# Softplus of the first two hidden tiles moved into the attention's list, splits and evictions reordered at a group change, and the last outputs written in another row order

## Chip, cores, metric

One core of a Trainium2 chip. The time is that of the device, in microseconds, from the start of the program to its end; a time below is the median of three runs. The engines named are PE (TensorE matmul) with its weight loads (PEld), DVE (VectorE), ACT (ScalarE), POOL (GpSimd) and SP (SyncE, which here issues nearly all the transfers).

## What is computed

```python
# q, k, v: 4 batches x 8 heads x 576 x 64, s: 4 x 8 x 576
scores = (q @ k.T) / 8 + min(-(cum[i] - cum[j]), 0)   # cum: running sum of max(s, 0)
x = softmax(causal(scores)) @ v                       # -> 2304 tokens x 512
h = x @ w_in;  x = softplus(h) @ w_out                # 512 -> 2048 -> 512
x = x / sqrt(mean(x * x) + 1e-6) * rms_g
g = x @ w_gate;  val = x @ w_val                      # 512 -> 1536
out = (g * sigmoid(g) * val) @ w_out2                 # 1536 -> 512, 2304 x 512 fp32
```

The products are kept near fp32 accuracy: an operand is split into a part `hi` rounded to fp32r and a rest `lo`, and a product is three matmuls (hi·hi, hi·lo, lo·hi). So every operand of TensorE costs one ACT copy (hi) and one subtraction on DVE or POOL (lo).

## The kernel before

**Three stages.** Attention runs over 16 pairs of heads. The first MLP runs over six tiles of 384 tokens and 16 slices of 128 hidden columns, 96 steps in all (`STEPS`, line 171). The second MLP runs over three groups of 768 tokens (two tiles of 384) and 12 slices of hidden columns, 36 steps in all; step n has group g = n // 12 and slice f = n % 12.

**Order of work.** Each engine takes its instructions strictly in the order in which they are written. For the attention that order comes from a planner: `attention_ops` (line 617) lists operations with engine, estimated duration and dependences, and `attention_order` (line 716) takes again and again the one that can start earliest, ties going to the lower rank (pair times a period plus an offset from the table `OFF`). The list ends with `H0` and `H1`, the first matmuls of the first MLP (`m1_h(0)`, `m1_h(1)`, lines 792 to 794), which write two PSUM banks of the attention's pool. From there on the order is a list of (time, function) pairs sorted by time. In it step i of the first MLP has `m1_h` (matmuls), `m1_sp` (two softplus activations of the same bank, `l` in fp32, line 813, and `gh` rounded, line 814), `m1_gl` (`gl` = `l` - `gh` on DVE, line 818) and `m1_y` (matmuls into four banks, line 830). The PSUM pool of the attention is closed and another opened in its place, so the banks of `y` lie over banks that the attention used.

**A step of the second MLP** is `m2_g(n)` (line 992). Gate and value of two token tiles are a 2 by 2 block product, made with seven products instead of eight (`prod`, six matmuls each, lines 979 to 981) in two PSUM banks D and A, in the order A12·B21 (D), A11·B11 (A), S2·T2 (A), S1·T1 (D), S3·T3 (A), S4·B22 (D), A22·T4 (A). The banks are read in between (`c1`, `u2`, `m5` on ACT; `gA`, `vB`, `gB` and the product with `s0` on DVE, line 1052), and the first product into a bank of the next step has to wait for the last read of it. The gated result is split by `m2_hi` (ACT, line 985) and `m2_lo` (DVE, line 990). `m2_out(n - 1, 0)` and `m2_out(n - 1, 1)` (line 1071, nine matmuls each) add the step before to six output banks: rows m = 0 to 2 of 128 tokens, then m = 3 to 5. `u_split` (lines 924, 925) splits the weights of the next step, one ACT copy and one POOL subtraction for each of four pieces. `u_load(n + 2)` (line 913) issues four loads on SP for the step after it; a load waits until POOL has done with the tile that it overwrites.

**At a group change** two things come on top. The seven token-side operands of the new group (B21, B11, T2, T1, T3, B22, T4, each in two halves j) are split by `n_split` (line 961): an ACT copy (line 968) and a subtraction (line 970), which is on POOL for an odd index and on DVE for an even one, so that of T1 the half j = 0 is POOL's and j = 1 DVE's. "ahead" is the last step of a group (n = 11, 23), "fresh" the first of the next (n = 12, 24). And the six output banks of the old group are copied out and stored by `m2_evac` (two copies of 256 columns and two stores on SP for each m). Its tiles in the first two groups are `yt`, of which there are seven that go round in order, `y_tile` at line 833. Before, the copies of m = 1, 3, 5 are ACT's (line 1082) and those of m = 0, 2, 4 DVE's (line 1084); rows 0 to 2 are copied in the fresh step, rows 3 to 5 in the one after it.

**At the end** `m2_end` (line 1087) adds the last two steps to the outputs and stores them, rows 0 to 2 first. There the even m use tiles `gl`, of which there are three.

Of the kernel before, what the change touches and what calls it, by code (L numbers as in the profile page):

```python
# [8 lines left out]
F32 = mybir.dt.float32  # L9
F32R = mybir.dt.float32r  # L10
# [5 lines left out]
ALU = mybir.AluOpType  # L16
# [96 lines left out]
    "X1": -56.86,  # L113
    "X2": 52.29,
    "X3": -59.99,
    "H0": -23.02,
    "H1": -64.43,
}
CONV0 = 7.439
CONVR = 1.0130  # L120
# [25 lines left out]
def attention_moe_kernel(ctx, tc, q, k, v, s, w_in, w_out, w_gate, w_val, w_out2, rms_g, out):  # L146
    nc = tc.nc
    B, H, S, D = q.shape
# [3 lines left out]
    P = 128  # L152
    NP = B * H // 2
    NH = B * H
    HP = H // 2
    KD = DM // P
    T = 384
# [8 lines left out]
    NA = 2 * FA  # L166
    CONV = [(1, c) for c in range(NA)]
    NG = NT // (2 * T)
    NS2 = NG * F2
    N5 = 3  # L170
    STEPS = [(t, t, f) for t in range(NTILE) for f in range(FA)]
# [8 lines left out]
    pools = {}  # L180
# [4 lines left out]
    def ps_p(name):  # L185
        return pools["ps"].tile([P, 512], F32, tag="p", name=name, bufs=2)
# [7 lines left out]
    def f32(ap):  # L194
        return ap.bitcast(F32)
# [96 lines left out]
    st = {}  # L292
# [324 lines left out]
    def attention_ops():  # L617
        ops, names = [], {}

        def op(name, eng, dur, fn, deps, base, lat=None, alloc=(), mode=""):  # L620
            if lat is None:
                lat = 0.3 if eng == "PE" else 0.15
            names[name] = len(ops)
            ops.append(dict(name=name, eng=eng, dur=dur, fn=fn, deps=deps, base=base, lat=lat, alloc=alloc, mode=mode))
# [82 lines left out]
            op((f"X{a}", 0), "DVE", 0.8, lambda a=a: x_split(0, a, nc.vector), [("XL", 0), ("QT1", NP - 1)] + [(f"X{a - 1}", 0)] * (a > 0), NP)  # L707
        for i in range(2):
            op((f"H{i}", 0), "PE", 2.1, lambda i=i: m1_h(i),
               [(f"X{a}", 0) for a in range(KD)] + [("MT", NP - 1), ("CL", NA - 1), ("CP", len(CONV) - 1)] + [("R" + x, p) for x in "abcd" for p in (NP - 2, NP - 1)], NP, mode="f")  # L710
        for o in ops:
            o["deps"] = [names[d] for d in o["deps"]]
            o["alloc"] = [(t, [names[r] for r in rd]) for t, rd in o["alloc"]]
# [92 lines left out]
    def m1_tile(tag, bufs, dt=F32):  # L806
        return pools["m1"].tile([P, T], dt, tag=tag, name=tag, bufs=bufs)

    def m1_sp(i):
        h = st.pop(("h", i))  # L810
        l = st["l", i] = m1_tile("l", 2)
        gh = st["gh", i] = m1_tile("gh", 3, F32R)
        nc.scalar.activation(out=l, in_=h, func=AF.Softplus)
        nc.scalar.activation(out=gh, in_=h, func=AF.Softplus)  # L814

    def m1_gl(i):
        gl = st["gl", i] = m1_tile("gl", 3, F32R)
        nc.vector.tensor_tensor(out=gl, in0=st.pop(("l", i)), in1=f32(st["gh", i]), op=ALU.subtract)  # L818

    def m1_y(i):  # L820
# [152 lines left out]
    def prod(o, n, wn, xn, start, stop):  # L973
        wh, wl = st["W", n, wn]
        for j in range(2):
            xh, xl = st["X", xn, j]
            c = slice(j * P, (j + 1) * P)
            first, last = start and j == 0, stop and j == 1
            nc.tensor.matmul(o, wh[:, c], xh, start=first, stop=False, skip_group_check=True)  # L979
            nc.tensor.matmul(o, wh[:, c], xl, start=False, stop=False, skip_group_check=True)  # L980
            nc.tensor.matmul(o, wl[:, c], xh, start=False, stop=last, skip_group_check=True)  # L981

    def m2_hi(n, h):
        gh, l = st["g", n][0], st["lt", n, h]
        nc.scalar.activation(out=gh[:, h * T:(h + 1) * T], in_=l, func=AF.Copy)

    def m2_lo(n, h):
        (gh, gl), l = st["g", n], st.pop(("lt", n, h))
        c = slice(h * T, (h + 1) * T)
        nc.vector.tensor_tensor(out=gl[:, c], in0=l, in1=f32(gh[:, c]), op=ALU.subtract)  # L990

    def m2_g(n, fill=None):
        g, f = divmod(n, F2)
        D, A = ps_p("D")[:, 0:T], ps_p("A")[:, 0:T]
        c1, u2, m5 = [m1_tile("gh", 3) for _ in range(3)]
        gA, s0, gB = [m1_tile("gl", 3) for _ in range(3)]
        s1, vB = m1_tile("u", 1), m1_tile("l", 2)
        st["g", n] = [pools["m1"].tile([P, 2 * T], F32R, tag="xb", name="gg", bufs=4) for _ in range(2)]
        tt, act = nc.vector.tensor_tensor, nc.scalar.activation
        ahead = f == F2 - 1 and g < NG - 1  # L1000
        fresh = f == 0 and g > 0

        def renew(go, *names):
            if go:
                for nm in names:
                    for j in range(2):
                        n_split(g + ahead, j, nm)

        prod(D, n, "A12", "B21", True, True)
        prod(A, n, "A11", "B11", True, False)  # L1010
        act(out=c1, in_=A, func=AF.Copy)
        if n:
            m2_hi(n - 1, 1)
            m2_lo(n - 1, 1)
        tt(out=gA, in0=D, in1=c1, op=ALU.add)
        act(out=s0, in_=gA, func=AF.Sigmoid)
        tt(out=s0, in0=gA, in1=s0, op=ALU.mult)
        if f == 1 and g > 0:
            m2_evac(g - 1, 1)
        if n:  # L1020
            m2_out(n - 1, 0)
        else:
            fill()
        renew(ahead, "B21", "B11")
        renew(fresh, "T1", "T3")
        if n == N5:
            m1_ssum(NTILE - 1, D)
            m1_ms(NTILE - 1)
        prod(A, n, "S2", "T2", False, False)
        act(out=u2, in_=A, func=AF.Copy)  # L1030
        renew(fresh, "B22")
        if n + 1 < NS2:
            u_split(n + 1, (0, 1))
        if 0 < n < NS2 - 1:
            m2_out(n - 1, 1)
        renew(ahead, "T2")
        prod(D, n, "S1", "T1", True, False)
        act(out=m5, in_=D, func=AF.Copy)
        renew(fresh, "T4")
        if fresh:  # L1040
            m2_evac(g - 1, 0)
        if n + 1 < NS2:
            u_split(n + 1, (2, 3))
        if n + 2 < NS2:
            u_load(n + 2)
        prod(A, n, "S3", "T3", False, False)
        tt(out=vB, in0=A, in1=m5, op=ALU.add)  # L1047
        prod(D, n, "S4", "B22", False, True)
        tt(out=gB, in0=D, in1=u2, op=ALU.add)
        act(out=s1, in_=gB, func=AF.Sigmoid)  # L1050
        prod(A, n, "A22", "T4", False, True)
        tt(out=s0, in0=A, in1=s0, op=ALU.mult)
        st["lt", n, 0], st["lt", n, 1] = s0, vB
        m2_hi(n, 0)
        tt(out=s1, in0=gB, in1=s1, op=ALU.mult)
        m2_lo(n, 0)
        tt(out=vB, in0=vB, in1=s1, op=ALU.mult)

    def m2_out(n, h):
        f = n % F2  # L1060
        if f == 0 and h == 0:
            st["o2"] = [ps_s("o") for _ in range(4)] + [ps_1("x1"), ps_1("o0")]
        w = slots[2, 3 * f + 2]
        gh, gl = st["g", n]
        ms = range(3 * h, 3 * h + 3)
        jobs = [(m, k) for k in range(3) for m in ms]
        if n == NS2 - 1:
            jobs = [(m, k) for m in ms for k in range(3)]
        for m, k in jobs:
            x, r = ((gh, w[0]), (gh, w[1]), (gl, w[0]))[k]  # L1070
            nc.tensor.matmul(st["o2"][m], x[:, m * P:(m + 1) * P], r, start=(f == 0 and k == 0),  # L1071
                             stop=(f == F2 - 1 and k == 2))

    def m2_evac(g, h):
        W = DM // 2
        for m in range(3 * h, 3 * h + 3):
            r = 2 * T * g + m * P
            for i, c in enumerate((slice(0, W), slice(W, DM))):
                ob = y_tile() if g < NG - 1 or m % 2 else m1_tile("gl", 3)
                ob, src = ob[:, 0:W], st["o2"][m][:, c]  # L1080
                if m % 2:
                    nc.scalar.activation(out=ob, in_=src, func=AF.Copy)  # L1082
                else:
                    nc.vector.tensor_copy(out=ob, in_=src)
                nc.sync.dma_start(out=out[r:r + P, c], in_=ob)

    def m2_end():
        n = NS2 - 1
        m2_out(n - 1, 1)
        m2_hi(n, 1)  # L1090
        m2_lo(n, 1)
        m2_out(n, 0)
        m2_evac(NG - 1, 0)
        m2_out(n, 1)
        m2_evac(NG - 1, 1)


    with tc.manual_schedule():
# [22 lines left out]
        with ExitStack() as es0:  # L1121
# [8 lines left out]
            NS = range(len(STEPS))  # L1130
            for i in NS:
                for nm, fn in (("h", m1_h), ("SP", m1_sp), ("GL", m1_gl), ("Y", m1_y)):
                    if (nm != "h" or i > 1) and (nm != "Y" or i + 1 < len(STEPS)):
                        at(i + OFF1[nm], fn, i)
            CONV1 = (("CF", w_fetch), ("CA", w_conv_a), ("CD", w_conv_d), ("CP", w_conv_p))
            SPLIT = (("CH", w_hi), ("CL", w_lo))
            x = OFF1["P0"]
# [11 lines left out]
            for v in sorted({STEPS[i][0] for i in NS}):  # L1149
                i = min(i for i in NS if STEPS[i][0] == v)  # L1150
                t, n = v % NTILE, FA if v < NTILE else F1 - FA
                if v > 0:
                    for a in range(KD):
                        x = i + OFF1["xs"] + OFF1["xt"] * a
# [3 lines left out]
                e = i + n - 1 + OFF1["Y"]  # L1158
# [7 lines left out]
                x = "5" if t == NTILE - 1 else ""  # L1166
# [9 lines left out]
            e = F1 * NTILE  # L1176
            F = OFF2["F"]

            for j in range(2):
                x = OFF2[f"x{j}"]  # L1180
# [13 lines left out]
            for n in range(NS2):  # L1194
                x = e + OFF2["g"] + F * n
                at(x, m2_g, n, m1_end if n == 0 else None)
            at(e + OFF2["g"] + F * NS2, m2_end)
            for g in range(1, NG):
                x = e + OFF2["g"] + F * F2 * (g - 1)
# [35 lines left out]
```

## Time and profile before

| | |
|---|---|
| median of 3 runs | 1062.54 us (1061.34 to 1063.38) |
| profiled execution, its own time | 1059.71 us |
| its span, first to last instruction | 1057.9 us |
| PE busy | 1029.3 us (97%) |
| DVE, ACT, POOL busy | 693.4, 540.6, 570.0 us (66%, 51%, 54%) |
| granted TensorE clock, mean | 0.998 |

A row of a timeline gives the start and the length in us, the engine, the line of the kernel, the operation, the tile written <- the tiles read, shapes, how many instructions are merged (x4), and in brackets the idle time of the engine before it and what ended it. PE is busy nearly all the time, so a change can gain by what is left of its waits and by the ends of the program.

### The profile page before, as it was taken

The numbers are of one execution on the slowest core, as the hardware profiler recorded it, in microseconds if no ns is written. First come the engines' busy times: TensorE is split into PE (matmuls) and PEld (weight loads), VectorE is DVE, ScalarE is ACT, GpSimd is POOL, SyncE is SP. The second block draws the span as 40 slices with busy tenths as digits, with TensorE's granted clock in tenths as the row PEclk, the third lists the DMA queues.
The fourth block names the chain that finished last, engine by engine and source line by source line (L and its number), as shares of the span: only waits on it lengthen the run. The fifth ranks groups of instructions, "written<-read, shape, count | busy, mean of one in ns | idle before, by whom it ended". The sixth has DMA issues, their size and how long they took to land.

```text
span 1057.9 us, 19448 instructions
## 1 busy us (share of the span) xinstructions
PE 1029.3 (97%) x7212; PEld 953.8 (90%) x7212; DVE 693.4 (66%) x1141; ACT 540.6 (51%) x1189; POOL 570.0 (54%) x477
## 2 busy tenths in 40 slices
PE   6999999999999999999999999999989999899997
PEld 5788877889999999999989998999979999799997
DVE  8888988418776756889898654545664346734444
ACT  2455666536656544544544544445554445644443
POOL 4378878736766433555767245355453433644331
PEclk9999999999999999999999999999999999999999
DMA  8367664345555575766542323224242233333221
GB/s 155 78 161 172 166 164 134 106 133 159 173 154 161 184 257 179 231 230 194 146 151 84 117 81 98 70 86 161 88 130 71 81 121 104 99 100 89 86 70 60
DMA packets 143758, 139.68 MB, mean 132 GB/s; under 512 B 68656, under 2 KB 118960, under 8 KB 143664
## 3 DMA queue, kind: packets, MB, share of 16 engines
q1 hardware_dynamic: 143632, 138.44, 44.5%
q8 instruction: 57, 0.93, 0.4%
q14 instruction: 37, 0.30, 0.1%
q0 software_dynamic: 32, 0.00, 0.0%
HBM read 106.73 MB, written 31.53 MB: 131 GB/s over the span
## 4 chain that ended last, share of the span: by engine, by line
PE 60%; DVE 7%; issue 3%; POOL 3%; DMA 2%; ACT 2%; SPq 0%; POOLq 0%; ACTq 0%; DVEq 0%
PE y L830 12%; PE o L1071 10%; PE A L979 4%; PE A L981 4%; PE A L980 4%; PE D L981 3%; PE D L979 3%; PE D L980 3%; PE h L792 3%; PE h L794 3%; PE h L793 3%; PE x L1071 2%; PE x L792 1%; PE x L794 1%; PE x L793 1%
## 5 line engine op out<-in xcount | busy, mean ns | idle before, releaser
L925 POOL TENSOR_TENSOR w<-wl,w 128x512 fp32r<-128x512 f32 x108 | 140.1, 1313 | 211.7 <-ACT w L924 211.7
L1071 PE MATMUL o<-w,gg 128*128 128x512 f32 x540 | 153.3, 393 | 0.3
L830 PE MATMUL y<-gh,w 128*128 128x384 f32 x768 | 149.8, 335 | 2.9 <-ACT gh L814 1.7
L830 PEld LDWEIGHTS y<-gh,w 128*128 128x128 f32 x768 | 134.4, 188 | 4.5 <-ACT gh L814 2.0
L1071 PEld LDWEIGHTS o<-w,gg 128*128 128x128 f32 x540 | 100.8, 188 | 19.4 <-ACT yt L1082 0.9
L979 PE MATMUL A<-xf,w 128*128 128x384 f32 x288 | 97.2, 338 | 6.2 <-DVE l L1047 4.7
L980 PE MATMUL A<-xf,w 128*128 128x384 f32 x288 | 96.9, 336 | 0.7 <-DVE xf L970 0.7
L981 PE MATMUL A<-xf,w 128*128 128x384 f32 x288 | 97.0, 337 | 0.0
L1047 DVE TENSOR_TENSOR l<-A,gh 128x384 f32<-128x384 f32 x36 | 20.0, 556 | 115.8 <-ACT w L924 113.3
L535 ACT ACTIVATE e<-t 128x448 f32<-128x448 f32 (+2 forms) x128 | 56.4, 505 | 71.3 <-PE t L528 66.4
L818 DVE TENSOR_TENSOR gl<-l,gh 128x384 fp32r<-128x384 f32 x96 | 79.3, 831 | 16.1 <-ACT gh L814 16.0
L261 POOL TENSOR_TENSOR wf<-ur 128x512 int32<-128x512 int32 x44 | 62.6, 1424 | 50.4 <-DVE ur L249 36.2
L485 DVE TENSOR_REDUCE mc<-s 128x2 f32<-128x512 f32 (+4 forms) x160 | 76.3, 534 | 19.0 <-PE s L470 15.0
L792 PE MATMUL h<-xh,w 128*128 128x384 f32 x256 | 85.6, 335 | 0.0
L793 PE MATMUL h<-xl,w 128*128 128x384 f32 x256 | 85.5, 334 | 0.0
L794 PE MATMUL h<-xh,w 128*128 128x384 f32 x256 | 85.5, 334 | 0.0
L830 PE MATMUL y<-gl,w 128*128 128x384 f32 x384 | 82.4, 335 | 2.3 <-DVE gl L818 2.2
L245 DVE TENSOR_SCALAR ur<-ur 128x512 f32<-128x512 f32 x68 | 51.3, 754 | 35.2 <-ACT ur L238 35.2
L979 PE MATMUL D<-xf,w 128*128 128x384 f32 x216 | 72.9, 338 | 0.0
L981 PE MATMUL D<-xf,w 128*128 128x384 f32 x216 | 72.8, 337 | 0.0
L980 PE MATMUL D<-xf,w 128*128 128x384 f32 x216 | 72.5, 336 | 0.0
L261 POOL TENSOR_TENSOR w<-ur 128x512 int32<-128x512 int32 x24 | 34.8, 1451 | 68.7 <-DVE ur L249 48.1
(171 smaller groups left out, 2662.8 us busy)
## 6 DMA issues: line engine op xcount, KB each, us to landing
wl<-wf SPq DMA_DIRECT2D x108, 256.0 KB
raw<-in_moe_w_out_dram SPq DMA_DIRECT2D x28, 512.0 KB
wf<-w SPq DMA_DIRECT2D x24, 512.0 KB
raw<-in_moe_w_in_dram SPq DMA_DIRECT2D x16, 512.0 KB
raw<-in_moe_w_gate_dram SPq DMA_DIRECT2D x12, 512.0 KB
raw<-in_moe_w_val_dram SPq DMA_DIRECT2D x12, 512.0 KB
xr<-x SPq DMA_DIRECT2D x28, 192.0 KB
qn<-in_q_dram SPq DMA_DIRECT2D x16, 288.0 KB
```

What stands on the lines that cost most here:

```text
L261: nc.gpsimd.tensor_tensor(out=w.bitcast(I32), in0=u, in1=r3, op=ALU.add)
L485: nc.vector.reduce_max(out=o, in_=x, axis=AX.X, negate=True)
L792: nc.tensor.matmul(o, wh, xh, start=start, stop=False)
L793: nc.tensor.matmul(o, wh, xl, start=False, stop=False)
L794: nc.tensor.matmul(o, wl, xh, start=False, stop=stop)
L818: nc.vector.tensor_tensor(out=gl, in0=st.pop(("l", i)), in1=f32(st["gh", i]), op=ALU.subtract)
L830: nc.tensor.matmul(y[m][:, 0:T], x[:, m * P:(m + 1) * P], r, start=first and x is w[0] and r is gh, stop=last and r is gl)
L925: nc.gpsimd.tensor_tensor(out=t[:, 1, 0:w], in0=src, in1=f32(t[:, 0, 0:w]), op=ALU.subtract)
L979: nc.tensor.matmul(o, wh[:, c], xh, start=first, stop=False, skip_group_check=True)
L980: nc.tensor.matmul(o, wh[:, c], xl, start=False, stop=False, skip_group_check=True)
L981: nc.tensor.matmul(o, wl[:, c], xh, start=False, stop=last, skip_group_check=True)
L1071: nc.tensor.matmul(st["o2"][m], x[:, m * P:(m + 1) * P], r, start=(f == 0 and k == 0), stop=(f == F2 - 1 and k == 2))
```

## The change

Three edits. (1) The two softplus activations and the subtraction of hidden tiles 0 and 1 are listed as operations `SP0`, `SP1` (ACT) and `SG0`, `SG1` (DVE) of the attention, after the exponentials of the last two pairs, with tiles from the attention's pools; H0 now comes before H1. (2) At a group change T1 is split in the last step of the old group, behind its last sigmoid; T3, B22 and T4 are split together early in the fresh step; all six rows are copied out in the fresh step, rows 0 and 2 where rows 0 to 2 were, rows 1, 3, 4, 5 behind the last sigmoid, with m = 1 and 3 on DVE and the rest on ACT. (3) At the end the products with `s1` go ahead of the one with `s0`, rows 3 to 5 are added and stored first, and each row is stored as soon as its own matmuls are done.

```diff
@@ attention_ops
-               [... H0 and H1 ...], NP, mode="f")
+               [... the same ...] + [("H0", 0)] * i, NP, mode="f")
+        for i in range(2):
+            op((f"SP{i}", 0), "ACT", 2.1 - 1.25 * i, lambda i=i: m1_sp(i), [(f"H{i}", 0)]
+               + [(f"E{x}{hd}", p) for x in "abcd" for hd in range(2) for p in (NP - 2, NP - 1)], NP)
+            op((f"SG{i}", 0), "DVE", 0.6, lambda i=i: m1_gl(i), [(f"SP{i}", 0)], NP)
@@ m1_sp
+        if i < 2:
+            if "l01" not in st:
+                st["l01"] = pools["e"].tile([P, 2, 1600], F32, tag="e", name="l")
+                st["g01"] = pools["split"].tile([P, 4, S], F32R, tag="hl", name="g", bufs=3)
+            l, gh = st["l", i], st["gh", i] = st["l01"][:, i, 0:T], st["g01"][:, i, 0:T]
+        else:
+            ...
@@ m1_gl
-        gl = st["gl", i] = m1_tile("gl", 3, F32R)
+        gl = st["gl", i] = m1_tile("gl", 3, F32R) if i > 1 else st["g01"][:, 2 + i, 0:T]
@@ m2_g
         tt(out=s0, in0=gA, in1=s0, op=ALU.mult)
-        if f == 1 and g > 0:
-            m2_evac(g - 1, 1)
         ...
         renew(ahead, "B21", "B11")
-        renew(fresh, "T1", "T3")
+        renew(fresh, "T3", "B22", "T4")
         ...
         prod(A, n, "S2", "T2", False, False)
         act(out=u2, in_=A, func=AF.Copy)
-        renew(fresh, "B22")
         ...
         act(out=m5, in_=D, func=AF.Copy)
-        renew(fresh, "T4")
         if fresh:
-            m2_evac(g - 1, 0)
+            m2_evac(g - 1, (0, 2))
         ...
         act(out=s1, in_=gB, func=AF.Sigmoid)
+        renew(ahead, "T1")
+        if fresh:
+            m2_evac(g - 1, (1, 3, 4, 5))
+        if n == NS2 - 1:
+            tt(out=s1, in0=gB, in1=s1, op=ALU.mult)
+            tt(out=vB, in0=vB, in1=s1, op=ALU.mult)
         prod(A, n, "A22", "T4", False, True)
         tt(out=s0, in0=A, in1=s0, op=ALU.mult)
         st["lt", n, 0], st["lt", n, 1] = s0, vB
-        m2_hi(n, 0)
         ...
+        if n < NS2 - 1:
+            m2_hi(n, 0)
+            ...
@@ m2_evac
-                if m % 2:
+                if m % 2 if g == NG - 1 else m not in (1, 3):
                     nc.scalar.activation(out=ob, in_=src, func=AF.Copy)
@@ m2_end
-        m2_out(n - 1, 1)
         m2_hi(n, 1)
         m2_lo(n, 1)
-        m2_out(n, 0)
-        m2_evac(NG - 1, 0)
-        m2_out(n, 1)
-        m2_evac(NG - 1, 1)
+        m2_hi(n, 0)
+        m2_lo(n, 0)
+        m2_out(n - 1, 1, (3, 4))
+        for m in (3, 4, 5, 0, 1, 2):
+            if m == 5:
+                m2_out(n - 1, 1, (5,))
+            m2_out(n, m // 3, (m,))
+            m2_evac(NG - 1, (m,))
```

## Rows read from the trace of the kernel before

**Rows 1.** The page, first part: busy us, share of the span, instructions.

```profile
PE 1029.3 (97%) x7212; PEld 953.8 (90%) x7212; DVE 693.4 (66%) x1141; ACT 540.6 (51%) x1189; POOL 570.0 (54%) x477
```

**Rows 2.** Waits of PE, whole span: us in total, times, longest us.

```profile
PE A L979 <- DVE l L1047: 4.7, 2, 2.4
```

**Rows 3.** Timeline of ACT at the end of the attention.

```profile
214.35 0.49 ACT L590 ACTIVATE xz<-o 128x384 f32<-128x384 f32 x1 [5.07 <-POOL zs L546]
...
221.42 1.28 ACT L813 ACT_TABLE_LOAD   x1
...
224.25 0.50 ACT L814 ACTIVATE gh<-h 128x384 fp32r<-128x384 f32 x1
```

**Rows 4.** Timeline of PE in the same stretch.

```profile
212.39 0.34 PE L794 MATMUL h<-xh,w 128*128 128x384 f32 x1
...
224.81 1.67 PE L830 MATMUL y<-gh,w 128*128 128x384 f32 x8 [1.66 <-ACT gh L814]
```

**Rows 5.** Timeline of PE at the first group change, steps 11 to 14.

```profile
753.16 2.24 PE L1071 MATMUL o<-w,gg 128*128 128x512 f32 x9
...
763.64 0.33 PE L979 MATMUL A<-xf,w 128*128 128x384 f32 x1
...
764.68 2.24 PE L1071 MATMUL o<-w,gg 128*128 128x512 f32 x9
...
776.41 0.41 PE L979 MATMUL A<-xf,w 128*128 128x384 f32 x1 [2.34 <-DVE l L1047]
...
779.61 2.24 PE L1071 MATMUL o<-w,gg 128*128 128x512 f32 x9
...
792.06 2.24 PE L1071 MATMUL o<-w,gg 128*128 128x512 f32 x9
```

**Rows 6.** Timeline of ACT at the same change.

```profile
755.91 1.75 ACT L968 ACTIVATE xf<-xs 128x384 fp32r<-128x384 f32 x4
...
762.35 0.53 ACT L1050 ACTIVATE u<-gl 128x384 f32<-128x384 f32 x1 [1.24 <-DVE gl L1049]
...
767.88 0.53 ACT L1016 ACTIVATE gl<-gl 128x384 f32<-128x384 f32 x1 [1.15 <-DVE gl L1015]
```

**Rows 7.** Timeline of DVE at the same change.

```profile
762.80 0.56 DVE L1052 TENSOR_TENSOR gl<-A,gl 128x384 f32<-128x384 f32 x1 [0.48 <-PE A L981]
763.27 1.41 DVE L1055 TENSOR_TENSOR u<-gl,u 128x384 f32<-128x384 f32 x1
...
769.26 3.64 DVE L970 TENSOR_TENSOR xf<-xs,xf 128x384 fp32r<-128x384 f32 x3 [0.27 <-ACT xf L968]
...
774.39 1.41 DVE L1084 COPY yt<-o 128x256 f32<-128x256 f32 x4
```

**Rows 8.** Timeline of POOL at the same change.

```profile
762.99 1.28 POOL L925 TENSOR_TENSOR w<-wl,w 128x512 fp32r<-128x512 f32 x1
...
770.13 2.36 POOL L970 TENSOR_TENSOR xf<-xs,xf 128x384 fp32r<-128x384 f32 x2 [0.22 <-PE o L1071]
...
776.51 1.29 POOL L925 TENSOR_TENSOR w<-wl,w 128x512 fp32r<-128x512 f32 x1
```

**Rows 9.** Timeline of SP's queue at the same change, the loads of step 14.

```profile
777.71 1.36 SPq L913 DMA_DIRECT2D wl<-wf  x3
```

**Rows 10.** The chain that ended last, in order of time, at the second change.

```profile
921.73 3.85 DMA xr<-wf
```

**Rows 11.** Timeline of SP's queue at the end.

```profile
1049.61 0.81 SPq L1085 DMA_DIRECT2D out_dram<-gl  x2
...
1054.45 0.90 SPq L1085 DMA_DIRECT2D out_dram<-yt  x2
```

**Rows 12.** The chain that ended last, at the end.

```profile
1049.61 1.72 DMA out_dram<-gl
```

**Rows 13.** Timelines of ACT and DVE at the end.

```profile
1045.44 0.53 ACT L1050 ACTIVATE u<-gl 128x384 f32<-128x384 f32 x1 [2.18 <-DVE gl L1049]
...
1051.42 0.42 DVE L1084 COPY gl<-o 128x256 f32<-128x256 f32 x1 [0.95 <-DMA out_dram<-gl]
```

More of the change, by code (lines that the diff above doesn't have):

```diff
@@ L115 @@
     "X3": -59.99,
-    "H0": -23.02,
-    "H1": -64.43,
+    "H0": -64.43,
+    "H1": -23.02,
+    "SP0": -60.0,
+    "SP1": -60.0,
+    "SG0": -60.0,
+    "SG1": -60.0,
 }
@@ L709, in attention_ops @@
             op((f"H{i}", 0), "PE", 2.1, lambda i=i: m1_h(i),
-               [(f"X{a}", 0) for a in range(KD)] + [("MT", NP - 1), ("CL", NA - 1), ("CP", len(CONV) - 1)] + [("R" + x, p) for x in "abcd" for p in (NP - 2, NP - 1)], NP, mode="f")
+               [(f"X{a}", 0) for a in range(KD)] + [("MT", NP - 1), ("CL", NA - 1), ("CP", len(CONV) - 1)] + [("R" + x, p) for x in "abcd" for p in (NP - 2, NP - 1)] + [("H0", 0)] * i, NP, mode="f")
+        for i in range(2):
+            op((f"SP{i}", 0), "ACT", 2.1 - 1.25 * i, lambda i=i: m1_sp(i), [(f"H{i}", 0)]
+               + [(f"E{x}{hd}", p) for x in "abcd" for hd in range(2) for p in (NP - 2, NP - 1)], NP)
+            op((f"SG{i}", 0), "DVE", 0.6, lambda i=i: m1_gl(i), [(f"SP{i}", 0)], NP)
         for o in ops:
@@ L810, in m1_sp @@
         h = st.pop(("h", i))
-        l = st["l", i] = m1_tile("l", 2)
-        gh = st["gh", i] = m1_tile("gh", 3, F32R)
+        if i < 2:
[4 more added lines that the diff above has]
+        else:
+            l = st["l", i] = m1_tile("l", 2)
+            gh = st["gh", i] = m1_tile("gh", 3, F32R)
         nc.scalar.activation(out=l, in_=h, func=AF.Softplus)
@@ L1053, in m2_g, with m2_out @@
         st["lt", n, 0], st["lt", n, 1] = s0, vB
-        m2_hi(n, 0)
[L1055 to L1059, printed above, removed]
+        if n < NS2 - 1:
+            m2_hi(n, 0)
+            tt(out=s1, in0=gB, in1=s1, op=ALU.mult)
+            m2_lo(n, 0)
+            tt(out=vB, in0=vB, in1=s1, op=ALU.mult)
+    def m2_out(n, h, ms=None):
         f = n % F2
@@ L1064, in m2_out @@
         gh, gl = st["g", n]
-        ms = range(3 * h, 3 * h + 3)
+        ms = range(3 * h, 3 * h + 3) if ms is None else ms
         jobs = [(m, k) for k in range(3) for m in ms]
-        if n == NS2 - 1:
-            jobs = [(m, k) for m in ms for k in range(3)]
         for m, k in jobs:
@@ L1072, in m2_out, with m2_evac @@
                              stop=(f == F2 - 1 and k == 2))
-    def m2_evac(g, h):
+    def m2_evac(g, ms):
         W = DM // 2
-        for m in range(3 * h, 3 * h + 3):
+        for m in ms:
             r = 2 * T * g + m * P
@@ L1088, in m2_end @@
         n = NS2 - 1
-        m2_out(n - 1, 1)
         m2_hi(n, 1)
         m2_lo(n, 1)
-        m2_out(n, 0)
-        m2_evac(NG - 1, 0)
-        m2_out(n, 1)
-        m2_evac(NG - 1, 1)
+        m2_hi(n, 0)
+        m2_lo(n, 0)
+        m2_out(n - 1, 1, (3, 4))
[4 more added lines that the diff above has]
+            m2_evac(NG - 1, (m,))
     with tc.manual_schedule():
@@ L1132, in attention_moe_kernel @@
                 for nm, fn in (("h", m1_h), ("SP", m1_sp), ("GL", m1_gl), ("Y", m1_y)):
-                    if (nm != "h" or i > 1) and (nm != "Y" or i + 1 < len(STEPS)):
+                    if (nm == "Y" or i > 1) and (nm != "Y" or i + 1 < len(STEPS)):
                         at(i + OFF1[nm], fn, i)
```

## The prediction

> **What bounds the kernel now.** I read the page first. PE is busy 97% of the span [rows 1], so a change can gain only where PE still waits, or after its last matmul. The waits of PE come next: the largest of the second MLP is on the DVE subtraction at line 1047, twice, 4.7 us together [rows 2]. Twice is the number of group changes. Then I read the timelines of the three places that the change touches.
>
> **Start.** ACT loads its table at 221.42 for 1.28 us, when the attention is over, and does the two softplus pairs only then; the last read of the second bank ends at 224.75 [rows 3]. PE begins `y` at 224.81, after 1.66 us idle [rows 4]. It waited for a bank that hidden tile 1 still held, not for operands. Ahead of this, ACT idles 5.07 us up to 214.35 [rows 3], while PE ends the second hidden tile at 212.73 [rows 4].
>
> **Group change.** `m2_out(n - 1, 0)` stands once in every step, so its starts measure the period: 753.16 to 764.68 is an undisturbed 11.52 us. The next two are 14.93 and 12.45 us [rows 5]. The change from group 0 to 1 thus costs 3.41 + 0.93 = 4.34 us; the second is taken as equal, since its wait is about the same [rows 2]. In the fresh step DVE does three subtractions in 3.64 us, a fourth, and four copies in 1.41 us, all ahead of line 1047 [rows 7]; PE waits 2.34 us for that line [rows 5].
>
> **End.** The first store is issued at 1049.61 and the twelfth is through at 1055.35, 0.48 us each without a break [rows 11]. SP's issuing sets the end.
>
> **Part 1, softplus early.** It removes nothing and moves four activations, one load and two subtractions into the idle ACT. Load 1.28 us, then the pairs (0.5 us each activation, [rows 3]); the second pair begins when PE ends at 212.73 and is over by about 213.8, before ACT's next work at 214.35. So the 1.66 us of PE go. DVE's two subtractions fall where nothing of the attention is due. No transfer is added. What the softplus gains passes on to the end if PE stays the bound in the first MLP. I take -1.7; bounds -1.7 and 0 (if another stop takes its place). The tiles borrowed from the attention's pools live until `y` of step 1; what the list lays over them is first written after that, so I cost it at nothing; without that cover the first splits of the weights would wait, and PE only if these came late in turn.
>
> In the trace the softplus follows the end of the load within the sum above, without a further stop. The Trainium skill, page "ScalarE: Activation LUTs", section "What ACT_TABLE_LOAD costs", gives 1.28 us for the load and 1.38 us more for a drain, 2.66 us a switch. By the page this part would be worth -3.0 and the whole sum would be -1.0; no such drain stands in the trace.
>
> **Part 2, T1 in the old group's last step.** The rows of step 11 in place: its last sigmoid starts at 762.35 and takes 0.53; T1's two copies follow at 0.44 each (four take 1.75), and the second ends near 763.8 [rows 6]. On DVE the subtraction of T1 (j = 1) now stands ahead of the product at line 1052. That product is the last read of bank A, now 762.80 to 763.36 [rows 7], and PE's A11·B11 of the next step, at 763.64 [rows 5], overwrites the bank. The subtraction costs between 0.56 (line 1052's own row) and 1.41 us, the length of the DVE row at 763.27 that ran beside POOL's at 762.99 [rows 7, 8]. I take 1.4, since it runs beside the same POOL row: it ends near 765.2, line 1052 at 765.7, and A11·B11 is 2.1 us late (1.2 at the lower bound).
>
> **Part 2, the fresh step.** DVE now has three subtractions ahead of line 1047 instead of four and four copies, and PE finds its banks read in time; the old 3.41 and 0.93 us go. What comes late next is another thing. The six rows take twelve copies in one step, and there are seven tiles `yt`. The twelfth (m = 5, second half, on ACT) must wait until the store of the fifth (m = 1, first half) has landed. That store is issued on SP behind the four loads of `u_load(14)`, the third of which waits for POOL to finish the third weight subtraction of this step. Behind the waiting copy on ACT stands `m2_hi(12, 0)`, and for that PE waits at `m2_out(12, 0)`. That seven tiles go round in order is no guess: at the end the fourth use of the three `gl` tiles waits 0.95 us for a store [rows 13].
>
> Worked out: line 1052 ends at 765.7; six more operations of about 0.55 us in turn on ACT and DVE (hi, lo, the other half's product, hi, lo, `gA`) bring the sigmoid to 769.2, against 767.88 before [rows 6]. With 0.53 for it and 0.88 for two copies of T3, POOL starts at about 770.6. Until its third weight subtraction is done it has the same six subtractions that it did before from 770.13 to 777.80, 7.67 us [rows 8]: 778.3. Two issues of 0.45 (three take 1.36, [rows 9]) bring SP to the store of m = 1 at 779.2. The store lands after 1.72 us, as at the end [rows 12], or up to 3.85 us, as the fourth load did at the second change, behind other transfers [rows 10]. I take 1.72, a store of the same size: 780.9. The copy (1.41/4 = 0.35, [rows 7]) and the split (0.53) end at 781.8. Undisturbed, `m2_out(12, 0)` would start at 776.2, so a change costs 5.6 us in place of 4.34: **+1.3 each, +2.6 for two.** Bounds of one: +0.4 (T1 at 0.56) and +3.4 (landing 3.85). SP's eight stores after it delay the loads of the step after, which have nearly a whole step.
>
> The 1.72 us is the time from issue to landing with nothing else in flight ahead. The Trainium skill, page "DMA: Bandwidth & Descriptors", in its table of two cost components, gives 2.0 us plus bytes over 436 GB/s, an estimate of 2.3 us for 128 KB. By the page a change would cost 0.6 more and the whole sum would be +1.6.
>
> **Part 3, the end.** The last sigmoid of gate starts at 1045.44 [rows 13]: 0.53 for it, 1.12 for two products, 0.53 and 0.56 for hi and lo, some 0.4 for the last matmul and 0.4 for the first copy give a first store near 1049.0 instead of 1049.61. A row's three matmuls take 0.75 (2.24 for nine, [rows 5]), less than its two issues (0.96), so SP stays the bound; row 5 comes after six matmuls and opens a small gap, and the last `gl` tile waits for a store again. I take -0.5; bounds -1.0 and 0.
>
> **Sum.** -1.7 + 2.6 - 0.5 = **+0.4 us**, made against the profiled execution's 1059.71, of which 1057.9 is span: 1060.1. The runs shown have their median 2.8 us higher, so the forecast is 1062.54 + 0.4 = **1062.9 us**, no change that can be told: a measurement of this kernel tells about 0.2%, 2.1 us. With the bounds of the parts the forecast's own range is 1060.6 to 1067.6 (-1.7 + 0.8 - 1.0 and -1.7 + 6.8 - 0).
>
> **Rivals.**
>
> *Faster: the wait for the output tile does not bind.* Then `m2_out(12, 0)` comes at 764.68 + 2.1 + 11.52 = 778.3, plus some 0.4 because line 1052 of the fresh step stands behind four DVE copies: a cost of 2.5 instead of 4.34, -1.8 each. Sum: -1.7 - 3.6 - 0.5 = -5.8, **1056.7 us**. It needs the store of m = 1 to land by about 777.5, when ACT comes to the twelfth copy. For it: before the change no `yt` tile was waited for. Against it: the order on SP, and 7.67 us of POOL's work ahead of the load that blocks it.
>
> *Slower: the landing takes as long as the loaded queue makes it.* The store of m = 1 goes out right behind two loads, 384 KB. At 3.85 us the change costs +3.4 each; sum -1.7 + 6.8 - 0.5 = +4.6, **1067.1 us**. It decides from a landing of about 2.6 us on, where the sum passes +2.1. For it: row 921.73 [rows 10]. Against it: that transfer is the fourth load of its step, with three of twice its size just ahead.
>
> *The softplus frees nothing at the start* (another bank is read at the same moment, or the first MLP's later DVE work takes the gain back): +2.1, **1064.6 us**. ACT's last reads of the attention are over long before 224.81, which speaks against it.
>
> **How the numbers follow.** Forecast 0.45, of which 0.37 falls within 0.2%, 0.02 below and 0.06 above; the tile's wait not binding 0.26, all faster; long landing 0.24, all slower; no gain at the start 0.05, all within. That makes 0.28 faster, 0.42 within 0.2%, 0.30 slower. The range goes from below the faster rival, with T1 at its lower bound (1056.0), to just above the slower one (1067.6); left out are changes that cost still more.
>
> **What would show it.** Right: the table load near 210, no idle PE before the first `y`; PE's A11·B11 of steps 12 and 24 waits for line 1052; ACT waits at line 1082 for a store, and PE at line 1071 for ACT in steps 13 and 25, some 5 us lost per change; the first store of the end half a microsecond earlier. Wrong: periods of `m2_out(n - 1, 0)` around a change that add up to less than 3 us over 11.52 each, or a wait of ACT there that names POOL or PE instead of a store.

## The result and the profile after

The median went from 1062.0 us (four runs, 1061.34 to 1063.38) to **1070.73 us** (four runs, 1069.92 to 1072.38): a ratio of **1.0083**, interval 1.0065 to 1.01, slower by 8.7 us. That is above the predicted range. The profiled execution has a span of 1068.1 us against 1057.9, and a mean granted clock of 0.992 against 0.998.

First the page's busy times and the waits of PE over the whole span (us in total, times, longest), which answer to [rows 1, 2]:

```profile
PE 1031.0 (97%) x7212; PEld 954.6 (89%) x7212; DVE 687.7 (64%) x1137; ACT 542.4 (51%) x1193; POOL 569.1 (53%) x477
```

```profile
PE o L1086 <- ACT gg L999: 10.4, 3, 5.1
...
PE A L993 <- DVE gl L1068: 3.4, 4, 1.4
PE y L844 <- DVE gl L832: 3.2, 3, 1.6
```

The busy times hardly moved. The wait of before (4.7 us behind line 1047) is gone, and two others stand in its place: the output matmuls wait for the split `m2_hi` (ACT, line 999), and the first product of a step waits for the product with `s0` (DVE, line 1068, once 1052). A third has grown: `y` waits 3.2 us for `m1_gl`, where it was 2.2.

PE's timeline at the start, at the first group change, at the stop of the second, and at the end (columns as in [rows 4, 5]):

```profile
220.67 0.45 PE L800 MATMUL x<-xh,w 128*128 128x384 f32 x1
...
222.86 2.24 PE L844 MATMUL y<-g,w 128*128 128x384 f32 x12
...
238.54 0.96 PE L844 MATMUL y<-gl,w 128*128 128x384 f32 x4 [1.65 <-DVE gl L832]
...
752.05 2.24 PE L1086 MATMUL o<-w,gg 128*128 128x512 f32 x9
...
764.08 0.45 PE L993 MATMUL A<-xf,w 128*128 128x384 f32 x1 [1.38 <-DVE gl L1068]
...
765.23 2.24 PE L1086 MATMUL o<-w,gg 128*128 128x512 f32 x9
...
783.05 4.21 PE L1086 MATMUL o<-w,gg 128*128 128x512 f32 x9 [5.10 <-ACT gg L999]
...
797.13 2.24 PE L1086 MATMUL o<-w,gg 128*128 128x512 f32 x9
...
931.30 4.17 PE L1086 MATMUL o<-w,gg 128*128 128x512 f32 x9 [4.76 <-ACT gg L999]
...
1055.57 0.39 PE L1086 MATMUL o<-w,gg 128*128 128x512 f32 x1
```

The four starts of `m2_out(n - 1, 0)` at the first change (752.05 to 797.13) give periods of 13.18, 17.82 and 14.08 us where an undisturbed one is 11.5. The first change costs 45.08 - 34.5 = **10.6 us**; before, the same three periods were 38.90 us, a cost of 4.4. The second, from starts at 900.63, 913.83, 931.30 and 944.73, costs **9.6**; before, its periods were 38.90 us too (895.77 to 934.67). Together the two changes lose 6.2 + 5.2 = 11.4 us. That is more than the whole span lost, 10.2: this execution came 0.9 us earlier to the second MLP (its first full output row at 647.89 instead of 648.82), and its other steps differ by a few tenths. The medians differ by less than the two spans, 8.7 us: the profiled execution of before is one of the faster of its kernel (1059.71 against a median of 1062.0).

Who is late, by ACT's timeline at the start and at the change [rows 3, 6], and the transfer that it names, by SP's timeline (the end of the program with it, [rows 9, 11]) and by the chain that ended last (start, us, what) at both changes [rows 10]:

```profile
208.47 1.28 ACT L827 ACT_TABLE_LOAD   x1
209.87 0.49 ACT L827 ACTIVATE l<-h 128x384 f32<-128x384 f32 x1
...
235.70 0.66 ACT L242 ACTIVATE ur<-raw 128x512 f32<-128x512 f32 x1 [7.61 <-DMA raw<-in_moe_w_in_dram]
...
782.21 0.38 ACT L1097 ACTIVATE yt<-o 128x256 f32<-128x256 f32 x1 [5.44 <-DMA out_dram<-yt]
```

```profile
226.99 4.29 SPq L618 DMA_DIRECT2D x<-xz  x2
231.32 0.43 SPq L231 DMA_DIRECT2D raw<-in_moe_w_in_dram  x1
...
773.11 1.80 SPq L1100 DMA_DIRECT2D out_dram<-yt  x4
775.01 2.13 SPq L927 DMA_DIRECT2D wl<-wf  x3
777.19 0.42 SPq L927 DMA_DIRECT2D xr<-wf  x1
777.71 5.24 SPq L1100 DMA_DIRECT2D out_dram<-yt  x8
...
1059.14 1.50 SPq L1100 DMA_DIRECT2D out_dram<-yt  x2
...
1064.67 0.89 SPq L1100 DMA_DIRECT2D out_dram<-gl  x2
```

```profile
775.53 1.28 POOL w L939
...
777.19 0.42 SPq L927
...
777.71 4.41 DMA out_dram<-yt
...
782.21 0.38 ACT yt L1097
782.59 0.42 ACT gg L999
...
783.05 4.21 PE o L1086 x9
...
926.29 4.08 DMA out_dram<-yt
```

The twelfth copy waits 5.44 us for a store. That store, the fifth of the twelve, goes out at 777.71 behind the four loads of step 14, and lands **4.41 us** after its issue (4.08 at the second change). The chain reads as it was written down: the third weight subtraction on POOL, the last load, the store, the twelfth copy, the split, the outputs.

The chain also holds a second loss: nine output matmuls take 4.21 us. The windows of the same stretch, with the granted clock (PEclk, 1.00 is 2.4 GHz, 0.50 is 1.2 GHz), show it:

```profile
core 0: us, PE busy (x) PEld busy (x) DVE busy (x) ACT busy (x) POOL busy (x), PEclk, DMA share, GB/s
...
780.00:781.00 1.00, 0.00 (x0) 0.00 (x0) 0.00 (x0) 0.00 (x0) 0.00 (x0) 1.00 1.04 365
781.00:782.00 1.00, 0.00 (x0) 0.00 (x0) 0.00 (x0) 0.00 (x0) 0.00 (x0) 0.85 0.94 325
...
787.00:788.00 1.00, 1.00 (x4) 0.94 (x3) 0.00 (x0) 0.00 (x0) 0.00 (x0) 0.50 0.00 0
788.00:789.00 1.00, 1.00 (x5) 0.96 (x5) 0.00 (x0) 0.03 (x1) 0.00 (x0) 0.74 0.00 0
```

PE does nothing from 777.95 on. Its clock is still full at 780, falls in the window 781 to 782, and stays at 0.50 up to 788, although PE works again from 783.05. The period from 783.05 has no other large stop and is 14.08 us: **2.6 us** lost to the clock after the wait itself is over (1.9 at the second change).

### The profile page after: what moved, and what is told of

It is laid out like the page before. It is cut to its first block, busy times and chain, and to the rows that moved or that the text cites. A ratio compares the mean times of both kernels' runs of the same rounds, so it can differ in the third digit from the quotient of the medians.

```text
span 1068.1 us, 19446 instructions
## 1 busy us (share of the span) xinstructions
PE 1031.0 (97%) x7212; PEld 954.6 (89%) x7212; DVE 687.7 (64%) x1137; ACT 542.4 (51%) x1193; POOL 569.1 (53%) x477
## 4 chain that ended last, share of the span: by engine, by line
PE 60%; DVE 7%; issue 4%; POOL 3%; DMA 2%; ACT 2%; SPq 0%; POOLq 0%; ACTq 0%; DVEq 0%
PE y L844 12%; PE o L1086 11%; PE A L993 4%; PE A L995 4%; PE A L994 4%; PE D L995 3%; PE D L993 3%; PE D L994 3%; PE h L801 3%; PE h L800 3%; PE h L802 3%; PE x L1086 2%; PE x L801 1%; PE x L800 1%; PE x L802 1%
## 5 line engine op out<-in xcount | busy, mean ns | idle before, releaser
L1086 PE MATMUL o<-w,gg 128*128 128x512 f32 x540 | 157.3, 402 | 10.4 <-ACT gg L999 10.4
L844 PE MATMUL y<-gh,w 128*128 128x384 f32 x752 | 146.6, 335 | 1.4 <-DVE yt L859 1.4
L844 PEld LDWEIGHTS y<-gh,w 128*128 128x128 f32 x752 | 131.7, 188 | 2.8 <-DVE yt L859 2.1
L1086 PEld LDWEIGHTS o<-w,gg 128*128 128x128 f32 x540 | 103.0, 192 | 30.9 <-ACT gg L999 11.4
L489 DVE TENSOR_REDUCE mc<-s 128x2 f32<-128x512 f32 (+4 forms) x160 | 76.3, 535 | 17.7 <-PE s L474 12.2
L832 DVE TENSOR_TENSOR gl<-l,gh 128x384 fp32r<-128x384 f32 x94 | 77.1, 826 | 15.4 <-ACT gh L828 15.2
L249 DVE TENSOR_SCALAR ur<-ur 128x512 f32<-128x512 f32 x68 | 54.0, 793 | 37.4 <-ACT ur L242 37.3
```

Source lines behind the costliest of these rows:

```text
L489: nc.vector.reduce_max(out=o, in_=x, axis=AX.X, negate=True)
L844: nc.tensor.matmul(y[m][:, 0:T], x[:, m * P:(m + 1) * P], r, start=first and x is w[0] and r is gh, stop=last and r is gl)
```

## The experiments

All kernels compute the whole of the reference. The kernel before was timed beside each group; rows that share its median ran on the same chip. The ratio is the recorded one, not the quotient of the two medians; the two differ by up to 0.0015 (twelfth_t1sig, whose six runs fall into four near 1055 and two near 1058.5).

| kernel | median us | before | ratio, 95% interval |
|---|---|---|---|
| start_only | 1061.10 | 1061.55 | 0.9999, 0.999 to 1.0008 |
| change_only | 1070.57 | 1061.55 | 1.0087, 1.0074 to 1.0101 |
| end_only | 1062.23 | 1061.55 | 1.0009, 1.0 to 1.0018 |
| twelfth_tile | 1055.41 | 1061.55 | 0.9944, 0.9931 to 0.9958 |
| t1_only | 1059.17 | 1061.34 | 0.9982, 0.9972 to 0.9992 |
| twelfth_t1back | 1057.67 | 1061.34 | 0.9963, 0.9951 to 0.9976 |
| twelfth_t1late | 1057.17 | 1061.34 | 0.9962, 0.9948 to 0.9976 |
| loads_last | 1058.01 | 1061.34 | 0.9969, 0.9958 to 0.9979 |
| twelfth_t1sig | 1055.34 | 1061.19 | 0.996, 0.9946 to 0.9975 |
| start_fetch | 1060.10 | 1061.19 | 0.9989, 0.9977 to 1.0002 |
| change_twelfth | 1055.78 | 1061.19 | 0.9952, 0.994 to 0.9964 |
| best | 1054.66 | 1061.19 | 0.9946, 0.9933 to 0.9959 |

### Each edit alone

**start_only**: the kernel before with edit (1).

```diff
+            op((f"SP{i}", 0), "ACT", 2.1 - 1.25 * i, lambda i=i: m1_sp(i), [(f"H{i}", 0)]
...
+            op((f"SG{i}", 0), "DVE", 0.6, lambda i=i: m1_gl(i), [(f"SP{i}", 0)], NP)
```

> The kernel before with the first edit alone (softplus of hidden tiles 0 and 1 in the attention's list). Theory: the first y matmul comes without the 1.66 us stop of PE, and of this about 0.9 us is left when the second MLP begins, as in the changed kernel, where the first output matmuls stand at 648.05 in place of 648.98: 0.9 us faster than before, a ratio of 0.999. Rival: the edit costs something elsewhere in the attention and the rest of the 8.8 us is partly its: then 0 or slower.

No difference: 0.9999. The stop before the first `y` is gone here too, but the next one is longer: 1.26 us before `y` of step 3, where the kernel before has 0.66.

**change_only**: the kernel before with edit (2).

```diff
-        renew(fresh, "T1", "T3")
+        renew(fresh, "T3", "B22", "T4")
...
+        renew(ahead, "T1")
+        if fresh:
+            m2_evac(g - 1, (1, 3, 4, 5))
```

> The kernel before with the second edit alone (splits and evictions at a group change). Theory: the whole loss is here: a group change costs about 10.6 and 9.6 us in the trace of the changed kernel in place of 4.3, so this is 11 to 12 us slower than before, about 1073.5, a ratio of 1.011. ACT waits 5 us at the twelfth copy for a store, and TensorE's granted clock falls to half behind that stop. Rival: the stop comes only together with the other edits: then within 3 us of before.

The whole loss is here, 1.0087 against 1.0083 for all three edits. Its output matmuls start at 752.35, 765.56, 783.32 and 797.32, with a stop of 5.04 us behind ACT's split: the same change as above, within 0.2 us in each period. By the medians it is 9.0 us slower, less than the 11 to 12 expected: those were read from the spans, against the profiled execution of before (1059.71).

**end_only**: the kernel before with edit (3).

```diff
-        m2_out(n, 0)
-        m2_evac(NG - 1, 0)
...
+        for m in (3, 4, 5, 0, 1, 2):
...
+            m2_evac(NG - 1, (m,))
```

> The kernel before with the third edit alone (rows 3 to 5 first at the end). From the last step's first output matmul to the end of the span the changed kernel takes 12.53 us, the one before 12.18. Theory: 0 to 0.4 us slower, no change that can be told. Rival (the prediction's): 0.5 us faster.

Nothing that can be told, if anything slower: 1.0009. From the first output matmul of `m2_end` to the end of the span it is 12.06 us, against 12.18 before.

### What the loss hangs on

**twelfth_tile**: the changed kernel, with the twelfth copy going to a tile that the second MLP does not use.

```diff
-                ob = y_tile() if g < NG - 1 or m % 2 else m1_tile("gl", 3)
+                ob = ss_tile("sh") if g < NG - 1 and m == 5 and i else y_tile() if g < NG - 1 or m % 2 else m1_tile("gl", 3)
```

> The changed kernel, with one difference: in the first two groups the twelfth copy (m = 5, second half) goes to a tile that nothing else uses in that step, in place of the eighth turn of the seven yt tiles. Theory (the stop is the store's landing): ACT's 5 us wait at that copy is gone, PE does not stop at the output matmuls, the clock stays at 1.0, and a group change costs 1.7 for T1 plus about 0.9: 2.6 in place of 10.1 on average, so about 15 us faster than the changed kernel, near 1055.5. Rival: the store's landing delays only that copy, and ACT or SP finds another stop of the same size behind it (a load, another tile): then the changed kernel's time less 1 to 3 us.

Two rows of its ACT timeline and PE's starts at the first change:

```profile
777.88 0.38 ACT L1097 ACTIVATE yt<-o 128x256 f32<-128x256 f32 x1
778.16 0.38 ACT L1097 ACTIVATE sh<-o 128x256 f32<-128x256 f32 x1
```

```profile
753.49 2.24 PE L1086 MATMUL o<-w,gg 128*128 128x512 f32 x9
...
766.70 2.24 PE L1086 MATMUL o<-w,gg 128*128 128x512 f32 x9
...
779.25 2.24 PE L1086 MATMUL o<-w,gg 128*128 128x512 f32 x9
...
790.78 2.24 PE L1086 MATMUL o<-w,gg 128*128 128x512 f32 x9
```

The copy no longer waits, the change costs 37.29 - 34.5 = 2.8 us in place of 10.6, the mean granted clock is 1.000, and the median falls from 1070.7 to 1055.4. One tile is worth 15 us. By the rows 7.8 us of them go at the first change: 17.82 - 12.55 = 5.27 in the period with the wait, and 14.08 - 11.53 = 2.55 in the one behind it, which is the clock's. At the second change it is 9.6 - 2.8 = 6.8.

**loads_last**: the changed kernel, with the loads of the fresh step issued behind the twelve stores instead of ahead of eight of them. All twelve copies keep to the seven `yt`.

```diff
-        if n + 2 < NS2:
+        if n + 2 < NS2 and not fresh:
...
             m2_evac(g - 1, (1, 3, 4, 5))
+            u_load(n + 2)
```

> The changed kernel with one difference: at a group change the four loads for step n + 2 are issued on SP behind the stores of rows 1, 3, 4, 5 in place of ahead of them; the seven tiles stay. Theory (what delays the store is the loads ahead of it, in SP's queue and on the transfer engines): the store of m = 1 is issued at about 775.2 in place of 777.7 and lands in 1.8 us in place of 4.4, before or within 0.5 us of ACT's twelfth copy; the 5 us stop and the clock's fall go. The loads come 2 to 3 us later than before: 1055 to 1058. Rival: eight stores ahead of the loads make the loads so late that ACT and PE stop in step n + 1: then little is won, 1062 to 1070.

Its SP queue (the second row is the fifth of the twelve stores by itself) and ACT at the first change:

```profile
775.22 5.81 SPq L1101 DMA_DIRECT2D out_dram<-yt  x12
777.27 0.33 SPq L1101 DMA_DIRECT2D out_dram<-yt  x1
781.13 1.37 SPq L927 DMA_DIRECT2D wl<-wf  x3
```

```profile
779.10 0.38 ACT L1098 ACTIVATE yt<-o 128x256 f32<-128x256 f32 x1 [0.22 <-DMA out_dram<-yt]
...
785.03 1.29 ACT L938 ACTIVATE w<-wl 128x512 fp32r<-128x512 f32 x2 [1.14 <-DMA wl<-wf]
```

The same copy into the same ring of seven waits 0.22 us instead of 5.44. From the store's issue at 777.27 to the copy it is 1.83 us; in the changed kernel it is 4.50 (777.71 to 782.21), 0.09 more than the landing of 4.41. So the store landed after about 1.7 us here, as in [rows 12]. It is the loads in flight ahead that make the landing long. That is half of the 5.2 us by which the wait shrank: the store also goes out 2.5 us earlier, 23.13 us behind the start of step 11's output matmuls (at 754.14) instead of 25.66. The later loads now cost ACT 1.14 us, which PE does not feel (the change costs 2.9).

**change_twelfth**: the kernel before, with edit (2) and the tile of twelfth_tile, so without edits (1) and (3).

```diff
...
+                ob = ss_tile("sh") if g < NG - 1 and m == 5 and i else y_tile() if g < NG - 1 or m % 2 else m1_tile("gl", 3)
```

> The kernel before with the group change's edit alone and the twelfth copy in another tile; softplus and end as before. Theory: the other two edits are worth nothing together (0.9999 and 1.0009 by themselves), so this gives the same as with all three, a ratio to before of 0.994 to 0.996. Rival: one of them is worth 1 us or more beside the other.

0.9952 against 0.9944 with all three edits, the intervals overlapping: edits (1) and (3) together show no gain that can be told.

### Where T1 belongs

**t1_only**: the kernel before, with T1 alone moved into the old group's last step.

```diff
-        renew(fresh, "T1", "T3")
+        renew(fresh, "T3")
...
         act(out=s1, in_=gB, func=AF.Sigmoid)
+        renew(ahead, "T1")
```

> The kernel before with only T1's split moved to the old group's last step, behind the last sigmoid; evictions and the other splits as before. Theory: DVE's subtraction of T1 ahead of the product that reads bank A last stops PE by 1.4 us and the step by 1.7, as in the changed kernel's trace (764.08, 1.38 idle; outputs at 765.23 in place of 763.55), and in the fresh step one subtraction less stands ahead of the DVE line that PE waits for, so that its 2.3 us stop falls to about 1.2: net 0.5 us slower a change, 0 to 2 us slower in all. Rival: T1 in the old step is free and the fresh step gains: 2 us faster.

PE's timeline at the first change:

```profile
765.75 0.44 PE L979 MATMUL A<-xf,w 128*128 128x384 f32 x1 [1.38 <-DVE gl L1053]
...
777.06 0.41 PE L979 MATMUL A<-xf,w 128*128 128x384 f32 x1 [1.61 <-DVE l L1047]
```

One stop of 2.34 us became two, of 1.38 and 1.61, and the change costs 4.5 us (starts 753.70 to 792.74), as before. Expected was 0 to 2 us slower; the medians are 2.2 us lower. What differs is the clock: its mean over an execution is 0.9985 averaged over the ten runs, and 0.9950 over the nineteen of the kernel before beside them. The kernels with the old group change lose clock at their own 2.3 us stop in some executions. The profiled execution that the prediction read lost none there (1.00, 4.4 us); start_only, whose group change is the old one, shows it at its first change (windows, columns as above):

```profile
774.00:776.00 2.00, 0.00 (x0) 0.00 (x0) 2.00 (x6) 0.77 (x2) 2.00 (x2) 1.00 0.19 63
776.00:778.00 2.00, 1.68 (x5) 1.71 (x6) 0.64 (x2) 0.52 (x1) 2.00 (x3) 0.55 0.80 264
778.00:780.00 2.00, 2.00 (x9) 2.00 (x8) 1.26 (x3) 0.53 (x1) 0.38 (x1) 0.60 0.69 138
```

That change costs 5.9 us, and the next one of the same execution, where the clock stays at 1.00, costs 4.4. Of the eight such stops in the profiled executions of before, start_only, end_only and start_fetch, four brought the clock to 0.50 (costs of 5.7 to 6.0 us) and four did not (4.4); in t1_only neither change did. That the two shorter stops keep the clock up is read from these means and rows; it wasn't tried by itself.

Three variants of twelfth_tile put T1 elsewhere: **twelfth_t1back** in the fresh step again, **twelfth_t1late** behind the products of the old step, **twelfth_t1sig** ahead of the last sigmoid.

```diff
-        renew(fresh, "T3", "B22", "T4")
+        renew(fresh, "T1", "T3", "B22", "T4")
...
-        renew(ahead, "T1")
```

> The kernel of the run with the twelfth copy in another tile, with T1's split back in the fresh step, in front of T3. Theory: the 1.7 us at the step's beginning go, but eight ACT copies in a row now delay u2 and m5, and four DVE subtractions the read of A: some 2.0 to 2.5 us a change instead of 2.8, so 0.5 to 1.5 us faster than that kernel, about 1054.5. Rival: T1's move was worth its price, the fresh step now costs 3 to 4 us: 1 to 2 us slower than it.

```diff
-        renew(ahead, "T1")
...
         st["lt", n, 0], st["lt", n, 1] = s0, vB
...
+        renew(ahead, "T1")
```

> The same kernel with T1's split in the old group's last step, but behind the step's last DVE product in place of ahead of the one that reads bank A. Theory: PE's stop of 1.4 us at A11 goes, the sigmoid of the fresh step is about 0.9 us late, u2 and m5 cost PE about 1.8: 2.2 us a change instead of 2.8, about 1 us faster, 1054.4. Rival: no difference, since DVE is the bound all through the fresh step.

```diff
-        act(out=s1, in_=gB, func=AF.Sigmoid)
         renew(ahead, "T1")
+        act(out=s1, in_=gB, func=AF.Sigmoid)
```

> The changed kernel with the twelfth copy in another tile, and T1's split written behind the last DVE sum and ahead of the last sigmoid of the old group's last step, in place of behind that sigmoid. Theory: ACT has 1.2 us idle there, the two copies fall into it, DVE's subtraction starts before bank A's last product is there, and PE's 1.4 us stop at A11 goes; a change costs about 1.2 us in place of 2.8: 1054 or less, a ratio to before near 0.993. Rival: the subtraction still delays the read of A by the time that POOL holds it up (0.5 us or more): no difference to the run with the twelfth copy alone.

The changes cost 2.3, 2.3 and 2.6 us in the profiled executions, against 2.8 in twelfth_tile. In the first two PE no longer stops 1.38 us at line 1068 but 1.0 us in the fresh step, for `u2` (ACT, line 1042), which stands behind the splits on ACT; in the third the two stops are 0.16 and 0.88 us. The ratios of all four overlap (0.9944 to 0.9963). So what T1's place is worth, a few tenths of a microsecond per change by the rows, is not told apart by the medians. The gains of about 1 us that were expected of these three did not show.

### Where the start's gain went

**start_fetch**: start_only, with the first two weight loads of the second phase issued in the attention's list.

```diff
+        for c in range(NA, NA + 2):
+            op(("CF", c), "SP", 0.65, lambda c=c: w_fetch(1, c), [("CD", c - 2)], CONV0 + CONVR * c, lat=6.0)
...
-                    at(x + OFF1[nm], fn, ph, c)
+                    if nm != "CF" or (ph, c) not in ((1, NA), (1, NA + 1)):
+                        at(x + OFF1[nm], fn, ph, c)
```

> The kernel with the softplus edit alone, and the two weight loads of the first MLP that ACT waits for near 236 issued in the attention's list, ahead of the attention's last stores. Theory (the edit's gain is lost there: PE stops 1.26 to 1.65 us at step 3 in place of 0.66, since ACT, in order, waits for a load that SP issued behind the last stores of the attention): the stop at step 3 goes, and 1 to 1.5 us against the kernel before are left. Rival: the gain is absorbed again where DVE is busy 90% of the time (446 to 578): no change.

ACT no longer waits for this weight; its timeline has the conversion without idle time ahead of it (7.23 us in start_only, 6.62 before):

```profile
229.09 0.66 ACT L242 ACTIVATE ur<-raw 128x512 f32<-128x512 f32 x1
```

The wait before `y` of step 3 is gone with it. From the first matmul of `H0` to the first full output row of the second MLP it is 438.4 us (208.79 to 647.19), against 440.55 in the kernel before and 439.9 in start_only. The medians say 0.9989, with 1 inside the interval: the rows show 1.5 us of gain over start_only in one execution, the times do not settle it.

**best**: twelfth_t1sig with these two loads issued early, so all three edits, the spare tile, and T1 ahead of the sigmoid.

```diff
...
+            op(("CF", c), "SP", 0.65, lambda c=c: w_fetch(1, c), [("CD", c - 2)], CONV0 + CONVR * c, lat=6.0)
```

> All three edits, the twelfth copy in another tile, T1's split ahead of the sigmoid, and the two loads issued early. Theory: the gains of the two add up, 8 to 9 us faster than before, a ratio near 0.992. Rival: the early loads are worth nothing: the same as the run with T1 ahead of the sigmoid.

It has the lowest median, 1054.66 us, and beats both kernels: 0.9946 of the kernel before, short of the 0.992 expected. It is not told apart from twelfth_tile or change_twelfth. The same stretch is 437.6 us here against 440.0 in twelfth_t1sig, but `H0` began 2.5 us later in its profiled execution (210.51 against 208.04); whether the early loads delay the attention stays open.

## Why the prediction was wrong, point by point

**Start, -1.7: right in place, worth 0.** The 1.66 us did go: from the first matmul of hidden tile 2 to `y` it is 2.19 us (220.67 to 222.86) against 4.02. But the stretch from `H0` to the second MLP is 440.44 us against 440.55. Of the 1.8 us freed, 0.7 went ahead of that point, between `H0` and tile 2 (13.22 us against 12.52), and 1.0 at step 3: PE's wait there grew from 0.66 to 1.65. ACT, in order, waits for a raw weight at 235.70, its softplus stands behind that, and SP issues the load at 231.32, behind the last stores of the attention, at a time that PE's gain does not move. The bound of 0 ("if another stop takes its place") held; the condition set for -1.7, that PE stays the bound in the first MLP, failed. start_fetch shows this wait: with the load issued earlier, the stop at step 3 is gone.

The Trainium skill, page "ScalarE: Activation LUTs", section "What ACT_TABLE_LOAD costs", gives 1.28 us and a drain of 1.38 more. The trace agrees with the first (1.28 at 208.47) and shows no drain: the softplus starts at 209.87, 0.12 us behind the load.

**T1, 2.1 us: 1.7.** DVE's timeline of the kernel after, at the end of step 11:

```profile
762.63 0.93 DVE L984 TENSOR_TENSOR xf<-xs,xf 128x384 fp32r<-128x384 f32 x1 [1.42 <-ACT xf L982]
763.48 0.54 DVE L1068 TENSOR_TENSOR gl<-A,gl 128x384 f32<-128x384 f32 x1
```

The subtraction took 0.93 us, not 1.4, between the two bounds; line 1068 follows it and PE's first product of step 12 follows that, as the working put them. The period is 13.18 us, 1.7 over 11.5.

**The wait for the tile: right in its mechanism, wrong in size.** The copy, the store that it waits for, the loads ahead of that store, and the split and PE behind it stand in the rows as predicted. Even the issue was within 0.4 us of its forecast place (25.66 us behind the start of step 11's output matmuls, 26.04 forecast). Some luck is in that: line 1068 ended 0.6 us earlier than forecast (11.97 us behind that start, not 12.54), and the way from there to the sigmoid took 0.5 us longer (4.0, not 3.5). **The step that failed is the sentence "the store lands after 1.72 us, as at the end"**: it landed after 4.41 and 4.08. The 1.72 was read at the end, with nothing in flight; here 896 KB of loads had been issued in the 2.7 us ahead, and the queues moved 365 GB/s in the window from 780, while PE, DVE, ACT and POOL all stood. Up to PE's restart the first change costs 783.05 - 752.05 - 23.04 = 8.0 us: the slower rival's 5.6 + 2.1 = 7.7, and a little more. The rival had the price; the argument against it, that row 921.73 was a fourth load behind three large ones, was no argument, since the store stands behind the same four.

The Trainium skill's page "DMA: Bandwidth & Descriptors", in its table of two cost components, led to an estimate of 2.3 us for this store. The trace does not agree: 4.41 and 4.08 with loads ahead, and about 1.7 without.

**The clock: no term held it.** A stop of 5 us brings the clock down to 0.50 (for some 6 us at the first change), and PE pays 2.6 and 1.9 us once it works again. That is nearly the whole distance between the slower rival's +3.4 a change and the measured +6.2 and +5.2, and about as much as the landing added (4.41 - 1.72 = 2.7, and 2.4 at the second change). The prediction also compared with a profiled execution in which the 2.3 us stop had kept its full clock, without asking whether that was the usual case; four of eight such stops in the profiled executions lost it.

**The end, -0.5: worth 0.** The first store is issued 3.57 us behind the first output matmul instead of 3.89, as forecast in direction. But SP's twelve issues then take 6.42 us (1059.14 to 1065.56) instead of 5.74: those of the first row alone take 1.50 us (0.81 in end_only; why is not shown). The small gap that row 5 was to open shows in end_only, 0.27 us. From the first output matmul of `m2_end` to the end it is 12.5 us, against 12.2 before and 12.1 in end_only.

**Sum.** By the rows: start -0.1, changes +11.4, end +0.3, against -1.7, +2.6 and -0.5. The slower rival was the right one, and was 3.6 us short. The faster rival, "the wait for the output tile does not bind", gave 1056.7 us: twelfth_tile, which makes it true, has 1055.4. The match is in part luck: by the rows its two changes save 3.2 us and its start and end nothing, where the rival counted 3.6 and 2.2; the rest of its 6.1 us is not in the rows, since the profiled execution of before had kept its clock. The foot of the prediction's range does not come out either: with T1 at its lower bound, 0.9 us a change less, the faster rival is at 1054.9, not at 1056.0.

## What to carry to other kernels

When copies of a burst outnumber the tiles they go to, the copying engine, and everything queued behind it, runs at the pace of the stores' landing: count the copies of the step against the ring, and give the last one a tile of its own if any lies idle. Read a transfer's landing time from a place where as much is in flight ahead of it as in the place to be forecast; a time read from an empty queue is a lower bound (here 1.7 us against 4.4). And price a long stop of PE twice: the stop itself, and the matmuls behind it at the lower clock.

## What the runs showed of the hardware that was not expected

The clock's fall outlasts the stop: in the change above PE works again from 783.05, and the clock is at 0.50 up to 788; nine matmuls took 4.21 us there, where the chain has 2.08 for the same nine at 752.21. A stop of 2.3 us does it in some executions and not in others of the same code (5.9 and 4.4 us for the two changes of one execution of start_only), and in t1_only, where two stops of 1.4 and 1.6 us stand in its place, the mean granted clock is 0.9985 instead of 0.9950. A 128 KB store takes 1.7 or 4.4 us from issue to landing, with nothing changed but the place of four loads in its queue (loads_last); the 4.4 lies beyond any bound in the prediction.
